# A tuned attention-and-GeGLU kernel on one core: tile 2's query transposes moved ahead of the first gates, one gate ahead of its value, and batch 2's attention one unit earlier

## Chip, cores, metric

One core of one Trainium2 chip. The metric is the device time of the kernel in microseconds (us). The traces also give the span from the first to the last instruction, which is about 2 us shorter than the time.

Engine names: PE is the matmul engine, DVE the vector engine, ACT the scalar engine, POOL and SP the two that here mostly issue or trigger transfers. A line such as L233 is a line of the kernel's source. In the views, `<-` in brackets names what ended a wait (its releaser), and DMA is a transfer between memories.

## The reference, cut

```python
# q, k, v: (8 batches, 8 heads, 576 positions, 64), float32
theta = pi / 2 * pos / S                       # S = 576
phi(x) = concat([relu(x) * cos(theta), relu(x) * sin(theta)])     # 128 features
kv  = phi(k)^T v ;  z = sum over positions of phi(k)              # per batch and head
out = (phi(q) kv) / (phi(q) z + 1e-6)
x   = out as (4608 tokens, 512)
y   = (gelu(x @ w_gate) * (x @ w_val)) @ w_out                    # d_ff = 1536
```

## The kernel before

The 4608 tokens are taken in nine blocks: block 0 is batch 0 (576 tokens), the others follow in steps of 512. A unit is one tile of 128 of the 1536 hidden columns: four gate matmuls, gelu on ACT, four value matmuls, and a product on DVE. Units are the time grid: block 1 (and each later one) has twelve, and between its units the next batch's attention is done. The kernel's PSUM is one tile, `ps`, of eight banks, and which bank a group uses is written by hand; so is the order of instructions on every engine.

```python
def norm(xb, bank, g0, g1, rows=128):          # numerator / denominator, all on DVE
    ... den = nd[..., D] + EPS                 # L181
    ... rec = 1 / den                          # L183
    ... xb[...] = nd[..., 0:D] * rec           # L184
def gate(n, jt, c0, w, gb):                    # L217: matmuls into bank gb; L222: gelu on ACT
def value(n, jt, c0, w, vb):                   # L228: matmuls into bank vb; L233: gel * value on DVE
def q_by_pe(b, j, bank, eng): ...              # L323: 8 transposes; L331/L333: copy to qT by eng
def x_by_pe(b, t, xb, bank, eng): ...          # L342: 4 transposes; L345: copy to xT by eng
def turn_x(b, t, xb): ...                      # L204: a DMA transposes xb into xT
def sq(j, which, eng): ...                     # L134 (DVE) or L136 (ACT): relu(q) * cos or sin
```

The start of block 0 (cut; "v" is DVE, "s" is ACT; X(t, bank, engine) is x_by_pe of tile t, Y(t, bank) its numerators and norm):

```python
    norm(x0, 6, 0, 1)
    dummies(1, 4)
    numer_mm(0, 0, 6, 1)
    norm(x0, 6, 1, 2)
    numer_mm(0, 1, 0, 0)
    numer_mm(0, 1, 0, 1)
    norm(x1, 0, 0, 2)
    x_by_pe(0, 0, x0, 4, "s", 0, 2)
    dummies(2, 5)
    x_by_pe(0, 0, x0, 4, "s", 2, 4)
    ...
    sq(2, 0, "v"), sq(2, 1, "s")
    gate(0, 0, 0, 128, 5)
    gate(0, 1, 0, 128, 4)
    X(1, 2, "s")()
    sq(3, 0, "v"), sq(3, 1, "v")
    dummies(1, 7)
    q_by_pe(0, 2, 3, "v")
    value(0, 0, 0, 128, 6)
    value(0, 1, 0, 128, 7)
    gate(0, 0, 128, 128, 5)
    gate(0, 1, 128, 128, 4)
    sq(4, 1, "s"), sq(4, 0, "v")
    q_by_pe(0, 3, 0, "s")
    value(0, 0, 128, 128, 6)
    value(0, 1, 128, 128, 7)
    Y(2, 2)()
    q_by_pe(0, 4, 1, "s")
    gv_unit(0, 2, *A, 4, 6)
    X(2, 0, "s")()
    ...
    X(4, 0, "v")()
    gv_unit(0, 4, *A, 3, 1)
    gv_unit(0, 2, *Bw, 4, 6)
    gv_unit(0, 3, *Bw, 5, 7)
    gv_unit(0, 0, 512, 64, 0, 3)
    gv_unit(0, 1, 512, 64, 1, 2)
```

Block 1 carries batch 2's attention (cut):

```python
    def attn_step(b, i):

        if i == 0:
            kv_half(b, 0, 6)
            kv_half(b, 1, 7)
        else:
            turn_x(b, i - 1, numer(b, i - 1, 6))
    ...
    # for n in 1..6, b = n + 1; put(u, ...) runs after unit u of block n
        put(0, L(sq, 0, 0, "v"), L(sq, 1, 0, "v"), L(sq, 1, 1, "v"), L(sq, 0, 1, "s"))
        put(1, L(sq, 2, 0, "v"), L(sq, 2, 1, "s"), L(turn_q, b, 0, 3))
        put(1, L(sq, 3, 0, "v"), L(sq, 4, 0, "v"), L(sq, 4, 1, "v"), L(sq, 3, 1, "s"), L(turn_q, b, 3, 5))
        put(2, L(sk, 0, 0, "v"), L(sk, 1, 0, "v"), L(sk, 0, 1, "s"), L(sk, 1, 1, "s"))
        put(3, L(sk, 2, 0, "v"), L(sk, 3, 0, "v"), L(sk, 4, 0, "v"))
        put(3, L(sk, 2, 1, "s"), L(sk, 3, 1, "s"), L(sk, 4, 1, "s"), L(cast_v, b, 0, 4))
        put(4, L(cast_v, b, 4, 8, "s"))
        put(5, L(attn_step, b, 0))
        ...
        for i in range(5):
            put(6 + i, L(attn_step, b, i + 1))
```

Of the kernel before, what the change touches and what calls it, by code (L numbers as in the profile page):

```python
# [16 lines left out]
def kernel(  # L17
# [19 lines left out]
    NJ = 4  # L37
# [86 lines left out]
    def dummies(n, bank=7):  # L124
        for _ in range(n):
            nc.tensor.matmul(ps[:, bank, :], lhsT=junk[:, 0:128], rhs=junk, start=True, stop=True)  # L126


    def scale(f, j, which, eng, h0=0, h1=H):
        dst, src = f  # L130
        col = (cos_c if which == 0 else sin_c)[:, j:j + 1]
        s, d = src[:, h0:h1, j, :], dst[:, j, h0:h1, which * D:(which + 1) * D]
        if eng == "v":
            nc.vector.tensor_scalar(d, s, col, 0.0, op0=ALU.mult, op1=ALU.max)  # L134
        else:
            nc.scalar.activation(d, s, AF.Relu, scale=col)  # L136
# [30 lines left out]
    def numer_mm(b, t, bank, g, rows=128):  # L167
        for h in range(4 * g, 4 * g + 4):
            nc.tensor.matmul(  # L169
                ps[0:rows, bank + g, (h % 4) * (D + 1):(h % 4 + 1) * (D + 1)],  # L170
                lhsT=qT[b % 2][:, t, h, 0:rows],
                rhs=kv[b % 2][:, h, 0:D + 1],
                start=True, stop=True,
            )

    def norm(xb, bank, g0, g1, rows=128):

        n = g1 - g0
        nd = ps[0:rows, bank + g0:bank + g1, 0:4 * (D + 1)].rearrange("p g (h e) -> p g h e", e=D + 1)
        den = rot.tile([128, 2, 4], FP32, name="den")  # L180
        nc.vector.tensor_scalar(den[0:rows, 0:n], nd[:, :, :, D], EPS, None, op0=ALU.add)  # L181
        rec = rot.tile([128, 2, 4], FP32, name="rec")
        nc.vector.reciprocal(rec[0:rows, 0:n], den[0:rows, 0:n])  # L183
        nc.vector.tensor_tensor(  # L184
            xb[0:rows, g0:g1], nd[:, :, :, 0:D],
            rec[0:rows, 0:n, :, None].to_broadcast([rows, n, 4, D]), op=ALU.mult,
        )
# [4 lines left out]
    def numer(b, t, bank, rows=128):  # L192

        numer_mm(b, t, bank, 0, rows)
        numer_mm(b, t, bank, 1, rows)
        xb = new_xb()
        norm(xb, bank, 0, 2, rows)
        return xb
# [14 lines left out]
    def gate(n, jt, c0, w, gb):  # L213

        p0 = starts[n] + c0
        for ct in range(CT):
            nc.tensor.matmul(  # L217
                ps[:, gb, 0:w], lhsT=wg_sb[:, ct, jt * 128:(jt + 1) * 128],
                rhs=xT[:, ct, p0:p0 + w], start=(ct == 0), stop=(ct == CT - 1),
            )  # L220
        gels[n, jt, c0] = gel = rot.tile([128, 512], FP32, name="gel", bufs=3)
        nc.scalar.activation(gel[:, 0:w], ps[:, gb, 0:w], AF.Gelu)  # L222

    def value(n, jt, c0, w, vb):

        p0 = starts[n] + c0
        for ct in range(CT):
            nc.tensor.matmul(  # L228
                ps[:, vb, 0:w], lhsT=wv_sb[:, ct, jt * 128:(jt + 1) * 128],
                rhs=xT[:, ct, p0:p0 + w], start=(ct == 0), stop=(ct == CT - 1),  # L230
            )
        gel = gels.pop((n, jt, c0))
        nc.vector.tensor_mul(hT[n % 2][:, jt, 64 + c0:64 + c0 + w], gel[:, 0:w], ps[:, vb, 0:w])  # L233

    def gv_unit(n, jt, c0, w, gb, vb, mid=()):
        gate(n, jt, c0, w, gb)
        for f in mid:
            f()
        value(n, jt, c0, w, vb)
# [15 lines left out]
    def o_part(n, m, bank, j0, j1):  # L255
        c0 = 128 * m - starts[n] + 64
        for jt in range(j0, j1):
            nc.tensor.matmul(  # L258
                ps[:, bank, :], lhsT=hT[n % 2][:, jt, c0:c0 + 128], rhs=wo_sb[:, jt, :],
                start=(jt == 0), stop=(jt == JT - 1),  # L260
            )
        if j1 == JT:
            o_store(m, bank)
# [21 lines left out]
    def o_store(m, bank):  # L285
        o_sb = rot.tile([128, C], FP32, name="o_sb", bufs=4)
        nc.scalar.copy(o_sb, ps[:, bank, :])  # L287
        if (128 * m) % S % 128 == 0 and (128 * m) % S < 512:
            nc.sync.dma_start(out=rows_ap(128 * m, 128), in_=o_sb)
        else:  # L290
            nc.sync.dma_start(out=rows_ap(128 * m, 64), in_=o_sb[0:64])
            nc.sync.dma_start(out=rows_ap(128 * m + 64, 64), in_=o_sb[64:128])
# [26 lines left out]
    def q_by_pe(b, j, bank, eng, h0=0, h1=H):  # L319

        qb = ps[:, bank, :].bitcast(BF16).rearrange("p (h t) -> p h t", h=H)
        for h in range(h0, h1):
            nc.tensor.transpose(out=qb[:, h, :], in_=qp[:, j, h, :], identity=ident)  # L323
        if eng is not None:
            q_evac(b, j, bank, eng, h0, h1)

    def q_evac(b, j, bank, eng, h0=0, h1=H):
        qb = ps[:, bank, :].bitcast(BF16).rearrange("p (h t) -> p h t", h=H)
        cp = nc.vector.tensor_copy if eng == "v" else nc.scalar.copy
        if j < NJ:  # L330
            cp(qT[b % 2][:, j, h0:h1], qb[:, h0:h1])  # L331
        else:
            cp(qT[b % 2][:, j, h0:h1, 0:64], qb[:, h0:h1, 0:128:2])  # L333

    def x_by_pe(b, t, xb, bank, eng, c0=0, c1=CT, every=1):
        p0 = b * S + t * 128
        cp = nc.vector.tensor_copy if eng == "v" else nc.scalar.copy
        xb2 = xb.rearrange("p g h d -> p (g h d)")
        rows = 128 if t < NJ or every == 2 else 64
        view = ps[:, bank, 0:256].bitcast(BF16).rearrange("p (c t) -> p c t", c=CT)  # L340
        for ct in range(c0, c1):
            nc.tensor.transpose(  # L342
                out=view[:, ct, 0:rows], in_=xb2[0:rows, ct * 128:(ct + 1) * 128], identity=ident[0:rows, 0:rows],
            )
        cp(xT[:, c0:c1, p0:p0 + rows // every], view[:, c0:c1, 0:rows:every])  # L345

    def sq(j, which, eng, *h):
        scale(Q, j, which, eng, *h)
# [30 lines left out]
    norm(x0, 6, 0, 1)  # L379
    dummies(1, 4)  # L380
    numer_mm(0, 0, 6, 1)
    norm(x0, 6, 1, 2)
    numer_mm(0, 1, 0, 0)
    numer_mm(0, 1, 0, 1)
    norm(x1, 0, 0, 2)
    x_by_pe(0, 0, x0, 4, "s", 0, 2)
    dummies(2, 5)
    x_by_pe(0, 0, x0, 4, "s", 2, 4)

    nc.gpsimd.tensor_copy(tiny[0:1, 1:2], x0[0:1, 1, 3, D - 1:D])  # L390
    load_w(8, 12)
# [2 lines left out]
    A, Bw = (0, 256), (256, 320)  # L394
    xs = {1: x1}

    def X(t, bank, eng):
        return lambda: x_by_pe(0, t, xs[t], bank, eng)

    def Y(t, bank):  # L400
        def f():
            xs[t] = numer(0, t, bank, 128 if t < NJ else 64)
        return f

    sq(2, 0, "v"), sq(2, 1, "s")
    gate(0, 0, 0, 128, 5)
    gate(0, 1, 0, 128, 4)
    X(1, 2, "s")()
    sq(3, 0, "v"), sq(3, 1, "v")
    dummies(1, 7)  # L410
    q_by_pe(0, 2, 3, "v")
    value(0, 0, 0, 128, 6)
    value(0, 1, 0, 128, 7)
    gate(0, 0, 128, 128, 5)
    gate(0, 1, 128, 128, 4)
    sq(4, 1, "s"), sq(4, 0, "v")
    q_by_pe(0, 3, 0, "s")
    value(0, 0, 128, 128, 6)
    value(0, 1, 128, 128, 7)
    Y(2, 2)()  # L420
    q_by_pe(0, 4, 1, "s")
    gv_unit(0, 2, *A, 4, 6)
    X(2, 0, "s")()
    Y(3, 2)()
# [5 lines left out]
    gv_unit(0, 0, 384, 128, 4, 6)  # L430
    gv_unit(0, 1, 384, 128, 5, 7)
    X(4, 0, "v")()
    gv_unit(0, 4, *A, 3, 1)
    gv_unit(0, 2, *Bw, 4, 6)
    gv_unit(0, 3, *Bw, 5, 7)
    gv_unit(0, 0, 512, 64, 0, 3)
    gv_unit(0, 1, 512, 64, 1, 2)


    load_q(1, nc.gpsimd)  # L440
# [7 lines left out]
    def L(f, *a):  # L448
        return lambda: f(*a)
# [54 lines left out]
    y4 = numer(1, 4, 0)  # L504
    o_part(0, 3, 5, 5, 10)
    x_by_pe(1, 3, y[3], 7, "s")
    o_part(0, 3, 5, 10, 12)
    x_by_pe(1, 4, y4, 6, "v", every=2)

    def attn_step(b, i):  # L510

# [8 lines left out]
    for n in range(1, 7):  # L520
        b = n + 1
        a = after[n]

        def put(u, *fs):
            a[u].extend(fs)

        put(0, L(sq, 0, 0, "v"), L(sq, 1, 0, "v"), L(sq, 1, 1, "v"), L(sq, 0, 1, "s"))
        put(1, L(sq, 2, 0, "v"), L(sq, 2, 1, "s"), L(turn_q, b, 0, 3))
        put(1, L(sq, 3, 0, "v"), L(sq, 4, 0, "v"), L(sq, 4, 1, "v"), L(sq, 3, 1, "s"), L(turn_q, b, 3, 5))
        put(2, L(sk, 0, 0, "v"), L(sk, 1, 0, "v"), L(sk, 0, 1, "s"), L(sk, 1, 1, "s"))  # L530
        put(3, L(sk, 2, 0, "v"), L(sk, 3, 0, "v"), L(sk, 4, 0, "v"))
        put(3, L(sk, 2, 1, "s"), L(sk, 3, 1, "s"), L(sk, 4, 1, "s"), L(cast_v, b, 0, 4))
        put(4, L(cast_v, b, 4, 8, "s"))
        put(5, L(attn_step, b, 0))
        if b + 1 < B:

            for f, u in zip((load_q, load_k, load_v), (3, 4, 5) if n > 1 else (6, 11, 11)):
                put(u, L(f, b + 1))
        for i in range(5):
            put(6 + i, L(attn_step, b, i + 1))  # L540

    for n in range(2, NB):
        for i, m in enumerate(o_tiles_of(n - 1)):
# [47 lines left out]
```

## Time and profile before

| | before |
|---|---|
| time, median of the first three runs | 329.17 us (328.63 to 329.31) |
| span in the trace | 326.8 us |
| PE busy / DVE / ACT | 97% / 53% / 46% |
| mean granted PE clock | 0.998 |
| PE's gaps in the list of waits | 4.3 us |

Two lines of the page: engines' busy time, and the chain that ended last.

```profile
PE 317.6 (97%) x2223; PEld 167.0 (51%) x2223; DVE 171.8 (53%) x382; ACT 150.6 (46%) x270; POOL 21.2 (6%) x41
...
PE 93%; DMA 3%; DVE 1%; ACT 1%; issue 1%; POOL 0%; SPq 0%; DVEq 0%; POOLq 0%; ACTq 0%
```

The kernel is bound by PE. The list of waits for PE in the kernel before (columns: line, what released it, total us, times, longest):

```profile
PE ps L126 <- DVE par_i L103: 1.7, 1, 1.7
PE ps L323 <- ACT qp L136: 1.0, 1, 1.0
PE ps L217 <- DMA xT<-xb: 0.8, 1, 0.8
PE ps L217 <- ACT xT L345: 0.3, 1, 0.3
PE ps L228 <- DVE hT L233: 0.2, 1, 0.2
PE ps L217 <- ACT gel L222: 0.2, 1, 0.2
```

The first two lie before 10 us and are not touched. The other four are 1.6 us together, so this change could reach only half a percent.

PE's timeline of the kernel before in block 0's beginning (start, duration, line, operation, matmuls in the group, and in brackets the idle time before it and its releaser):

```profile
15.64 0.28 PE L342 MATMUL ps<-ident,xb 128*128 128x128 bf16 x2
15.76 0.28 PE L217 MATMUL ps<-xT,wg_sb 128*128 128x128 bf16 x2
16.38 0.49 PE L217 MATMUL ps<-xT,wg_sb 128*128 128x128 bf16 x6 [0.35 <-ACT xT L345]
...
16.94 0.38 PE L126 MATMUL ps<-junk 128*128 128x512 bf16 x1
17.16 0.61 PE L323 MATMUL ps<-ident,qp 128*128 128x128 bf16 x8
...
18.05 0.61 PE L217 MATMUL ps<-xT,wg_sb 128*128 128x128 bf16 x8
18.50 0.61 PE L323 MATMUL ps<-ident,qp 128*128 128x128 bf16 x8
18.94 0.61 PE L228 MATMUL ps<-xT,wv_sb 128*128 128x128 bf16 x8
19.39 0.42 PE L169 MATMUL ps<-kv,qT 128*128 128x65 bf16 x8
```

How to read it: a group's duration runs to the modelled end of its last matmul, so groups overlap. The start-to-start distance is what counts. Eight 128-column matmuls take 18.50 - 18.05 = 0.45 us here, 56 ns each; twelve of 512 columns take 2.59 us elsewhere (306.43 to 309.02 us), 216 ns each. A single 512-column matmul is shown with 379 ns (the page's mean for L258), and the eight 128-column ones with 0.61 us. So about 0.16 us (379 - 216 ns, 0.61 - 0.45 us) of a gap behind such a group is hidden in the list of waits, and the list also leaves out what is then under 0.15 us.

PE's timeline of the kernel before at the end of block 1:

```profile
80.98 0.42 PE L169 MATMUL ps<-kv,qT 128*128 128x65 bf16 x8
...
82.10 1.03 PE L228 MATMUL ps<-xT,wv_sb 128*128 128x512 bf16 x4
83.97 1.02 PE L217 MATMUL ps<-xT,wg_sb 128*128 128x512 bf16 x4 [0.85 <-DMA xT<-xb]
```

Block 2's first gate waits until 83.97 for the DMA that turns batch 2's tile 3 (issued at 80.96, landed at 83.84 in the trace).

### The profile page before, as it was taken

To read this page: it belongs to the slowest core of one execution; us is meant where nothing else is said; L and a number is where in the kernel's file an instruction comes from. 1 tells how busy PE (TensorE), PEld (TensorE's weight loads), DVE (VectorE), ACT (ScalarE), POOL (GpSimd) and SP (SyncE) were. 2 spreads that over 40 slices of the span, in tenths; PEclk is the share of its full clock that TensorE was granted. 3 is DMA by queue.
4 is the path that set the end of the run, shared out by engine and by line. 5 is a ranking of instruction groups with operands and counts; after the bars stand their busy time and mean duration, and the time that the engine had idled before them with its cause. 6 is when DMAs were issued, how large, how long until landed. Compare 5 with 4: busy or idle time off the path is not lost.

```text
span 326.8 us, 5867 instructions
## 1 busy us (share of the span) xinstructions
PE 317.6 (97%) x2223; PEld 167.0 (51%) x2223; DVE 171.8 (53%) x382; ACT 150.6 (46%) x270; POOL 21.2 (6%) x41
## 2 busy tenths in 40 slices
PE   7799999999899999999999999999999999999994
PEld 3497866555345544544454445444544444444443
DVE  5894776678753667365835484548455222322210
ACT  6574664772474256424652375237622332223321
POOL 2640010000100010001000010001000100100000
PEclk9999999999999999999999999999999999999999
DMA  7999999997699948993699359994523211000024
GB/s 226 284 205 275 205 298 306 316 182 173 189 270 270 299 103 158 301 267 81 129 305 290 81 101 216 357 135 84 144 51 79 44 37 34 32 32 32 35 64 96
DMA packets 87739, 55.42 MB, mean 170 GB/s; under 512 B 52512, under 2 KB 82976, under 8 KB 87712
## 3 DMA queue, kind: packets, MB, share of 16 engines
q1 hardware_dynamic: 81200, 48.71, 60.2%
q0 software_dynamic: 6080, 5.90, 10.1%
q10 hardware_dynamic: 432, 0.46, 0.4%
q8 instruction: 17, 0.28, 0.4%
q14 instruction: 10, 0.08, 0.1%
HBM read 37.75 MB, written 9.44 MB: 144 GB/s over the span
## 4 chain that ended last, share of the span: by engine, by line
PE 93%; DMA 3%; DVE 1%; ACT 1%; issue 1%; POOL 0%; SPq 0%; DVEq 0%; POOLq 0%; ACTq 0%
PE ps L217 28%; PE ps L228 28%; PE ps L258 28%; PE ps L169 3%; PE ps L153 3%; DMA qf<-in_q_dram 2%; PE ps L323 1%; DMA xT<-xb 1%; PE ps L342 1%; PE ps L276 1%; DVE vx L140 0%; SPq L79 0%; DVE hT L233 0%; DVE qT L331 0%; DVE xb L184 0%
## 5 line engine op out<-in xcount | busy, mean ns | idle before, releaser
L233 DVE TENSOR_TENSOR hT<-gel,ps 128x512 bf16<-128x512 f32 (+5 forms) x126 | 76.4, 610 | 129.4 <-PE ps L228 127.8
L217 PE MATMUL ps<-xT,wg_sb 128*128 128x512 bf16 (+5 forms) x504 | 113.7, 348 | 1.4 <-DMA xT<-xb 0.8
L228 PE MATMUL ps<-xT,wv_sb 128*128 128x512 bf16 (+5 forms) x504 | 113.6, 349 | 0.2 <-DVE hT L233 0.2
L222 ACT ACTIVATE gel<-ps 128x512 f32<-128x512 f32 (+5 forms) x126 | 67.5, 536 | 77.6 <-PE ps L217 75.7
L258 PE MATMUL ps<-wo_sb,hT 128*128 128x512 bf16 x420 | 96.5, 379 | 0.0
L228 PEld LDWEIGHTS <-wv_sb 128*128 128x128 bf16 x504 | 47.8, 98 | 46.4 <-issue 0.4
L217 PEld LDWEIGHTS <-wg_sb 128*128 128x128 bf16 x504 | 45.8, 98 | 41.8 <-issue 2.1
L258 PEld LDWEIGHTS <-hT 128*128 128x128 bf16 x420 | 40.0, 98 | 45.4
L287 ACT COPY o_sb<-ps 128x512 f32<-128x512 f32 x35 | 20.5, 586 | 75.2 <-PE ps L258 75.2
L184 DVE TENSOR_TENSOR xb<-ps,rec 128x512 bf16<-128x512 f32 (+2 forms) x41 | 27.8, 678 | 1.7 <-DVE rec L183 0.2
L136 ACT ACTIVATE kp<-kf,sin_c 128x512 bf16<-128x512 f32 (+1 forms) x41 | 25.4, 679 | 0.4 <-DMA kf<-in_k_dram 0.4
L134 DVE TENSOR_SCALAR qp<-qf,cos_c 128x512 bf16<-128x512 f32 x40 | 20.5, 553 | 0.0
L169 PEld LDWEIGHTS <-qT 128*128 128x128 bf16 (+1 forms) x320 | 15.0, 98 | 8.7 <-issue 1.9
L134 DVE TENSOR_SCALAR kp<-kf,cos_c 128x512 bf16<-128x512 f32 (+1 forms) x45 | 18.7, 463 | 1.0 <-DMA kf<-in_k_dram 1.0
L136 ACT ACTIVATE qp<-qf,sin_c 128x512 bf16<-128x512 f32 x27 | 18.5, 712 | 0.0
L169 PE MATMUL ps<-kv,qT 128*128 128x65 bf16 (+1 forms) x320 | 16.5, 193 | 0.2
L208 POOL COPY xT<-xr 128x256 bf16<-128x256 bf16 x6 | 2.4, 403 | 201.0 <-DMA xr<-xb 201.0
L153 PEld LDWEIGHTS <-kp 128*128 128x128 bf16 x320 | 10.9, 97 | 2.6 <-issue 0.7
L126 PE MATMUL ps<-junk 128*128 128x512 bf16 x35 | 9.9, 424 | 1.7 <-DVE par_i L103 1.7
L153 PE MATMUL ps<-vx,kp 128*128 128x65 bf16 x320 | 11.1, 193 | 0.1
L140 ACT CAST vx<-vf 128x1280 bf16<-128x1280 f32 (+1 forms) x9 | 9.7, 1074 | 1.2 <-DMA vf<-in_v_dram 1.2
L244 POOL COPY hT<-hT 128x768 bf16<-128x768 bf16 x8 | 7.6, 948 | 36.8 <-DVE hT L233 36.8
(55 smaller groups left out, 88.9 us busy)
## 6 DMA issues: line engine op xcount, KB each, us to landing
out_dram<-o_sb SPq DMA_DIRECT2D x38, 128.0 KB, 2.4
kf<-in_k_dram SPq DMA_DIRECT2D x7, 640.0 KB, 7.5
out_dram<-o_sb SPq DMA_DIRECT2D x16, 256.0 KB, 3.4
qf<-in_q_dram SPq DMA_DIRECT2D x6, 640.0 KB, 6.2
vf<-in_v_dram SPq DMA_DIRECT2D x6, 640.0 KB, 9.1
kf<-in_k_dram SPq DMA_DIRECT2D x7, 512.0 KB, 6.4
qf<-in_q_dram SPq DMA_DIRECT2D x6, 512.0 KB, 5.4
vf<-in_v_dram SPq DMA_DIRECT2D x6, 512.0 KB, 8.0
```

Source lines behind the costliest of these rows:

```text
L126: nc.tensor.matmul(ps[:, bank, :], lhsT=junk[:, 0:128], rhs=junk, start=True, stop=True)
L134: nc.vector.tensor_scalar(d, s, col, 0.0, op0=ALU.mult, op1=ALU.max)
L136: nc.scalar.activation(d, s, AF.Relu, scale=col)
L153: nc.tensor.matmul(ps[:, bank, (h % 4) * (D + 1):(h % 4 + 1) * (D + 1)], lhsT=kp[:, j, h, :], rhs=vx[b % 2][:, j, h, 0:D + 1], start=(j == ...
L169: nc.tensor.matmul(ps[0:rows, bank + g, (h % 4) * (D + 1):(h % 4 + 1) * (D + 1)], lhsT=qT[b % 2][:, t, h, 0:rows], rhs=kv[b % 2][:, h, 0:D ...
L184: nc.vector.tensor_tensor(xb[0:rows, g0:g1], nd[:, :, :, 0:D], rec[0:rows, 0:n, :, None].to_broadcast([rows, n, 4, D]), op=ALU.mult,)
L217: nc.tensor.matmul(ps[:, gb, 0:w], lhsT=wg_sb[:, ct, jt * 128:(jt + 1) * 128], rhs=xT[:, ct, p0:p0 + w], start=(ct == 0), stop=(ct == CT - 1),
L222: nc.scalar.activation(gel[:, 0:w], ps[:, gb, 0:w], AF.Gelu)
L228: nc.tensor.matmul(ps[:, vb, 0:w], lhsT=wv_sb[:, ct, jt * 128:(jt + 1) * 128], rhs=xT[:, ct, p0:p0 + w], start=(ct == 0), stop=(ct == CT - 1),
L233: nc.vector.tensor_mul(hT[n % 2][:, jt, 64 + c0:64 + c0 + w], gel[:, 0:w], ps[:, vb, 0:w])
L258: nc.tensor.matmul(ps[:, bank, :], lhsT=hT[n % 2][:, jt, c0:c0 + 128], rhs=wo_sb[:, jt, :], start=(jt == 0), stop=(jt == JT - 1),)
L287: nc.scalar.copy(o_sb, ps[:, bank, :])
```

## The change

Three things are meant. (1) In block 0, tile 2's eight query transposes fill the wait before the first gate's second half, and a dummy matmul goes. For that the scalings of tile 2 go ahead of tile 1's norm; two copies and a scaling change engines. (2) The gate of hidden tile 4 goes ahead of its value and of two other units, and some units use other banks. (3) Six of batch 2's ten q scalings go ahead of block 1, and all its attention one unit sooner (s = -1).

```diff
--- before.py
+++ after.py
@@ -379,13 +379,16 @@
     norm(x0, 6, 0, 1)
     dummies(1, 4)
     numer_mm(0, 0, 6, 1)
+    sq(2, 1, "s")
     norm(x0, 6, 1, 2)
+    sq(2, 0, "v")
     numer_mm(0, 1, 0, 0)
     numer_mm(0, 1, 0, 1)
     norm(x1, 0, 0, 2)
     x_by_pe(0, 0, x0, 4, "s", 0, 2)
     dummies(2, 5)
     x_by_pe(0, 0, x0, 4, "s", 2, 4)
+    q_by_pe(0, 2, 3, None)
 
     nc.gpsimd.tensor_copy(tiny[0:1, 1:2], x0[0:1, 1, 3, D - 1:D])
     load_w(8, 12)
@@ -402,23 +405,21 @@
             xs[t] = numer(0, t, bank, 128 if t < NJ else 64)
         return f
 
-    sq(2, 0, "v"), sq(2, 1, "s")
     gate(0, 0, 0, 128, 5)
     gate(0, 1, 0, 128, 4)
-    X(1, 2, "s")()
-    sq(3, 0, "v"), sq(3, 1, "v")
-    dummies(1, 7)
-    q_by_pe(0, 2, 3, "v")
+    X(1, 2, "v")()
+    q_evac(0, 2, 3, "v")
+    sq(3, 0, "v"), sq(3, 1, "s")
     value(0, 0, 0, 128, 6)
     value(0, 1, 0, 128, 7)
     gate(0, 0, 128, 128, 5)
     gate(0, 1, 128, 128, 4)
     sq(4, 1, "s"), sq(4, 0, "v")
-    q_by_pe(0, 3, 0, "s")
     value(0, 0, 128, 128, 6)
     value(0, 1, 128, 128, 7)
     Y(2, 2)()
-    q_by_pe(0, 4, 1, "s")
+    q_by_pe(0, 3, 0, "s")
+    q_by_pe(0, 4, 1, "v")
     gv_unit(0, 2, *A, 4, 6)
     X(2, 0, "s")()
     Y(3, 2)()
@@ -430,11 +431,12 @@
     gv_unit(0, 0, 384, 128, 4, 6)
     gv_unit(0, 1, 384, 128, 5, 7)
     X(4, 0, "v")()
-    gv_unit(0, 4, *A, 3, 1)
+    gate(0, 4, *A, 3)
     gv_unit(0, 2, *Bw, 4, 6)
     gv_unit(0, 3, *Bw, 5, 7)
-    gv_unit(0, 0, 512, 64, 0, 3)
-    gv_unit(0, 1, 512, 64, 1, 2)
+    value(0, 4, *A, 1)
+    gv_unit(0, 0, 512, 64, 0, 2)
+    gv_unit(0, 1, 512, 64, 4, 6)
 
 
     load_q(1, nc.gpsimd)
@@ -504,8 +506,11 @@
     y4 = numer(1, 4, 0)
     o_part(0, 3, 5, 5, 10)
     x_by_pe(1, 3, y[3], 7, "s")
+    x_by_pe(1, 4, y4, 6, "v", every=2)
+    for j in range(NJ + 1):
+        sq(j, 0, "v")
     o_part(0, 3, 5, 10, 12)
-    x_by_pe(1, 4, y4, 6, "v", every=2)
+    sq(0, 1, "s")
 
     def attn_step(b, i):
 
@@ -524,20 +529,25 @@
         def put(u, *fs):
             a[u].extend(fs)
 
-        put(0, L(sq, 0, 0, "v"), L(sq, 1, 0, "v"), L(sq, 1, 1, "v"), L(sq, 0, 1, "s"))
-        put(1, L(sq, 2, 0, "v"), L(sq, 2, 1, "s"), L(turn_q, b, 0, 3))
-        put(1, L(sq, 3, 0, "v"), L(sq, 4, 0, "v"), L(sq, 4, 1, "v"), L(sq, 3, 1, "s"), L(turn_q, b, 3, 5))
-        put(2, L(sk, 0, 0, "v"), L(sk, 1, 0, "v"), L(sk, 0, 1, "s"), L(sk, 1, 1, "s"))
-        put(3, L(sk, 2, 0, "v"), L(sk, 3, 0, "v"), L(sk, 4, 0, "v"))
-        put(3, L(sk, 2, 1, "s"), L(sk, 3, 1, "s"), L(sk, 4, 1, "s"), L(cast_v, b, 0, 4))
-        put(4, L(cast_v, b, 4, 8, "s"))
-        put(5, L(attn_step, b, 0))
+        s = 0 if n > 1 else -1
+        if n > 1:
+            put(0, L(sq, 0, 0, "v"), L(sq, 1, 0, "v"), L(sq, 1, 1, "v"), L(sq, 0, 1, "s"))
+            put(1, L(sq, 2, 0, "v"), L(sq, 2, 1, "s"), L(turn_q, b, 0, 3))
+            put(1, L(sq, 3, 0, "v"), L(sq, 4, 0, "v"), L(sq, 4, 1, "v"), L(sq, 3, 1, "s"), L(turn_q, b, 3, 5))
+        else:
+            put(0, L(sq, 1, 1, "s"), L(sq, 2, 1, "v"), L(turn_q, b, 0, 3))
+            put(0, L(sq, 3, 1, "v"), L(sq, 4, 1, "s"), L(turn_q, b, 3, 5))
+        put(2 + s, L(sk, 0, 0, "v"), L(sk, 1, 0, "v"), L(sk, 0, 1, "s"), L(sk, 1, 1, "s"))
+        put(3 + s, L(sk, 2, 0, "v"), L(sk, 3, 0, "v"), L(sk, 4, 0, "v"))
+        put(3 + s, L(sk, 2, 1, "s"), L(sk, 3, 1, "s"), L(sk, 4, 1, "s"), L(cast_v, b, 0, 4))
+        put(4 + s, L(cast_v, b, 4, 8, "s"))
+        put(5 + s, L(attn_step, b, 0))
         if b + 1 < B:
 
-            for f, u in zip((load_q, load_k, load_v), (3, 4, 5) if n > 1 else (6, 11, 11)):
+            for f, u in zip((load_q, load_k, load_v), (3, 4, 5) if n > 1 else (5, 10, 11)):
                 put(u, L(f, b + 1))
         for i in range(5):
-            put(6 + i, L(attn_step, b, i + 1))
+            put(6 + s + i, L(attn_step, b, i + 1))
 
     for n in range(2, NB):
         for i, m in enumerate(o_tiles_of(n - 1)):
```

## The prediction

> **What bounds the kernel.** TensorE. The page gives PE 97% busy (317.6 of 326.8 us), the chain of waits is 93% PE, granted clock 0.998, DVE 53%, ACT 46%. [...] I use waits and start-to-start distances: almost everywhere PE's groups follow at a steady pitch (0.86 us per four 512-column matmuls). The list of waits gives PE 4.3 us of gaps: 1.7 and 1.0 before 10 us, which stay, and 0.35 (gate on ACT's copy into xT, 16.4 us), 0.24 (value on DVE's product, 25.2), 0.20 (gate on gelu, 29.6) and 0.85 (block 2's first gate, 84.0, on the DMA that turns batch 2's tile 3 into xT). So about 1.6 us, 0.5%, is all the change can reach, plus one dummy matmul.
>
> **What it does.** No real matmul goes; one 128x512 dummy does (0.22 us of pitch).
>
> 1. *Block 1 to 2.* Six q scalings of batch 2 (five on DVE at 0.40 us, one on ACT at 0.62) move ahead of block 1; all its attention runs one unit earlier (2.0 us of PE). Tile 3's transpose, issued at 80.96 and landed at 83.84 against a gate that could start at 83.12, would land near 81.9 against a gate near 82.9. The 0.85 us goes whole. Inputs allow it: q landed at 56.07, k at 60.07, v at 63.25. ACT is nearly packed from 62.5 to 70.4; its last v cast ends near 68.3 against a need near 68.9, DVE's near 67.8 against 68.3: margins of about 0.5 us. The last x tile, turned before two output matmuls, waits for its DVE product: cost about 0.1.
>
> 2. *First gates.* Tile 2's eight transposes (0.44 us) fill the 0.35 us wait; with the dummy a gain of about 0.5. But DVE runs packed there (14.0 to 25.4 with 0.34 us idle) and gets tile 1's xT copy (0.36) and tile 4's q copy (0.35) for one scaling (0.40). It waits for tile 1's transposes after a product that slipped 0.4; the first value product starts near 18.9 instead of 18.45. The second pair of values (banks 6 and 7) waits about 0.7 us on DVE, where tile 3's q transposes no longer fill. The wait at 25.2 grows to about 0.4. Net 0 to +0.3 us, I take +0.15.
>
> 3. *Gate (0,4) ahead of its value* covers the last xT copy (0.3 us); new banks trade the 0.20 at 29.6 for a wait on the late product (0.15). Net 0.
>
> Sum: -0.85 +0.10 +0.15 = -0.6 us; if the early part gains as meant, up to -1.6. All of it is on the chain, since PE is.
>
> **Prediction.** 328.4 us, 80% between 327.5 and 329.2. Faster by over 2%: 0.01; within 2%: 0.98; slower: 0.01.
>
> **Signs.** PE's list of waits no longer shows a gate on the DMA near 83 us; tile 3's transpose is issued about 2 us earlier; block 2 starts 0.6 to 1.0 us sooner; from there PE's groups are shifted by a constant. The wait at 16.4 is gone, and PE waits on DVE show near 19 (value) and 25.6. The first 256-column gate starts at 20.3 to 20.9 (before 20.21).
>
> **What would make it wrong.** The DVE wait near 19 may be smaller (then -1.3 or better). Batch 2's key-value halves may wait for casts, or qT's transposes, issued while v and outputs still land, may be late for the numerators near 71 (up to 1 us). q's second load landed at 14.27, just when ACT now wants it.

## The result

The first comparison gave 328.98 us (328.39 to 329.42, 4 runs) against 328.90 us (328.51 to 329.31, 4 runs). The ratio is 1.0001, with a 95% interval of 0.9979 to 1.0023: the same. Ratios here are the mean time of one kernel's runs over that of the other's of the same rounds, so they are not quite the ratio of the medians quoted.

The same lines of the page of the changed kernel, and its list of PE's waits:

```profile
PE 316.8 (97%) x2188; PEld 167.4 (51%) x2222; DVE 172.1 (53%) x383; ACT 150.4 (46%) x269; POOL 21.5 (7%) x41
...
PE 91%; DVE 3%; DMA 2%; issue 1%; SPq 1%; POOL 0%; ACT 0%; DVEq 0%; POOLq 0%
```

```profile
PE ps L126 <- DVE par_i L103: 1.7, 1, 1.7
PE ps L228 <- DVE hT L233: 0.8, 2, 0.6
PE ps L153 <- DVE vx L140: 0.4, 2, 0.3
PE ps L169 <- DVE xb L184: 0.3, 1, 0.3
```

Every wait that the change aimed at in block 2 and at the first gate is gone, and the list is shorter. (The missing 1.0 us of L323 and the new 0.4 us of L153 lie before 13.3 us, which the change does not touch; they come and go between traces. The changed kernel's second trace has 0.63 us of L323 again.) Yet the span is 326.7 us. PE's timeline of the changed kernel, the same places:

```profile
15.76 0.28 PE L342 MATMUL ps<-ident,xb 128*128 128x128 bf16 x2
16.14 0.62 PE L323 MATMUL ps<-ident,qp 128*128 128x128 bf16 x8
16.60 0.61 PE L217 MATMUL ps<-xT,wg_sb 128*128 128x128 bf16 x8
17.18 0.40 PE L342 MATMUL ps<-ident,xb 128*128 128x128 bf16 x4
17.41 0.61 PE L228 MATMUL ps<-xT,wv_sb 128*128 128x128 bf16 x8
18.09 0.62 PE L217 MATMUL ps<-xT,wg_sb 128*128 128x128 bf16 x8
19.28 0.61 PE L228 MATMUL ps<-xT,wv_sb 128*128 128x128 bf16 x8 [0.56 <-DVE hT L233]
19.72 0.42 PE L169 MATMUL ps<-kv,qT 128*128 128x65 bf16 x8
```

```profile
71.75 0.42 PE L169 MATMUL ps<-kv,qT 128*128 128x65 bf16 x8
...
72.87 1.03 PE L228 MATMUL ps<-xT,wv_sb 128*128 128x512 bf16 x4
74.17 0.42 PE L169 MATMUL ps<-kv,qT 128*128 128x65 bf16 x8 [0.28 <-DVE xb L184]
...
80.18 0.42 PE L169 MATMUL ps<-kv,qT 128*128 128x65 bf16 x8
...
82.16 1.03 PE L217 MATMUL ps<-xT,wg_sb 128*128 128x512 bf16 x4
...
83.89 1.03 PE L217 MATMUL ps<-xT,wg_sb 128*128 128x512 bf16 x4
```

The last gate in the second list is block 2's first one, at 83.89 us instead of 83.97: the block starts on time for its data, but no earlier.

I cut the trace at three points: the start of the second key-value half (PE, near 13.1 us), the start of hidden tile 4's 320-column gate in block 0 (the "wide gate"; first gate after the four 64-column groups), and block 2's first gate. The start point differs by up to 0.5 us between runs (12.8 to 13.3 us, by the span less the three distances). It needs the casts of v, and these v's landing: in the changed kernel DVE's second cast starts at 12.58 us after a 0.31 us wait for v's DMA, and the half at 13.20 after a 0.27 us wait for that cast. So I compare distances:

| kernel | A: key-value half to wide gate | B: wide gate to block 2 | C: block 2 to end | span |
|---|---|---|---|---|
| before | 16.57 | 54.32 | 242.81 | 326.8 |
| changed | 17.00 | 53.69 | 242.81 | 326.7 |

The change loses 0.43 us in A, gains 0.63 us in B, and nothing differs in C. The first point lay 0.12 us later in the changed kernel's run.

Where A is lost. Between 15.76 and 19.72 us PE does eight transposes and a dummy less than before (0.45 + 0.22 us), but takes 3.96 us instead of 3.75. Its start-to-start gaps are 0.27 us at 16.14, 0.13 at 17.18, 0.24 at 18.09 and 0.74 at 19.28: 1.38 us in all, against 0.51 at 16.38 before. The list of waits shows only 0.56 of it. DVE of the changed kernel in this stretch:

```profile
15.61 0.48 DVE L134 TENSOR_SCALAR qp<-qf,cos_c 128x512 bf16<-128x512 f32 x1
...
16.43 0.69 DVE L184 TENSOR_TENSOR xb<-ps,rec 128x512 bf16<-128x512 f32 x1
17.61 0.42 DVE L345 COPY xT<-ps 128x512 bf16<-128x512 bf16 x1 [0.49 <-PE ps L342]
17.95 0.68 DVE L331 COPY qT<-ps 128x1024 bf16<-128x1024 bf16 x1
18.55 0.47 DVE L134 TENSOR_SCALAR qp<-qf,cos_c 128x512 bf16<-128x512 f32 x1
18.95 0.47 DVE L233 TENSOR_TENSOR hT<-gel,ps 128x128 bf16<-128x128 f32 x2
```

All four gaps end with DVE. The scaling of tile 2, which now stands ahead of tile 1's norm, ends at 16.09 and releases the transposes at 16.14. The norm behind it ends at 17.12 (before: 16.62) and releases tile 1's transposes at 17.18. DVE then idles 0.49 us for these transposes; its copy into xT ends at 18.04 and releases the gate at 18.09. It copies and scales once more, and only then makes the product, at 18.95 (before: 18.45), which frees the bank that the value group at 19.28 writes.

So the filled wait did not become shorter: the first three gaps are 0.64 us, where 0.51 stood. The sum for A is +0.13 for these, +0.74 for the value group, -0.22 for the dummy, and -0.22 for smaller gaps after 19.4 us: +0.43.

Where B stays short of 0.85 us. The DMA wait went, but a numerator group at 74.17 now waits 0.28 us for DVE's division. DVE's product of the unit before, which the division follows, started at 72.39, though the record of its wait for PE ended at 71.97 and its gelu at 71.68. This 0.42 us pause had no cause in any semaphore that the trace shows.

### The profile page after: what moved, and what is told of

It is laid out like the page before. It is cut to its first block, busy times and chain, and to the rows that moved or that the text cites. A ratio compares the mean times of both kernels' runs of the same rounds, so it can differ in the third digit from the quotient of the medians.

```text
span 326.7 us, 5828 instructions
## 1 busy us (share of the span) xinstructions
PE 316.8 (97%) x2188; PEld 167.4 (51%) x2222; DVE 172.1 (53%) x383; ACT 150.4 (46%) x269; POOL 21.5 (7%) x41
## 4 chain that ended last, share of the span: by engine, by line
PE 91%; DVE 3%; DMA 2%; issue 1%; SPq 1%; POOL 0%; ACT 0%; DVEq 0%; POOLq 0%
PE ps L217 28%; PE ps L258 28%; PE ps L228 27%; PE ps L169 3%; PE ps L153 3%; DMA vf<-in_v_dram 2%; SPq L79 1%; DVE hT L233 1%; PE ps L276 1%; PE ps L342 1%; PE ps L323 1%; DVE xb L184 1%; DVE qp L134 0%; DVE rec L183 0%; DVE vx L140 0%
## 5 line engine op out<-in xcount | busy, mean ns | idle before, releaser
L228 PE MATMUL ps<-xT,wv_sb 128*128 128x512 bf16 (+5 forms) x492 | 111.8, 348 | 1.1 <-DVE hT L233 0.8
L217 PE MATMUL ps<-xT,wg_sb 128*128 128x512 bf16 (+5 forms) x490 | 111.8, 348 | 1.0
L258 PE MATMUL ps<-wo_sb,hT 128*128 128x512 bf16 x413 | 95.5, 379 | 0.6
L136 ACT ACTIVATE qp<-qf,sin_c 128x512 bf16<-128x512 f32 x28 | 19.3, 713 | 0.2 <-DMA qf<-in_q_dram 0.2
L153 PEld LDWEIGHTS <-kp 128*128 128x128 bf16 x320 | 10.9, 97 | 2.9 <-issue 1.0
L153 PE MATMUL ps<-vx,kp 128*128 128x65 bf16 x320 | 11.1, 193 | 0.4 <-DVE vx L140 0.4
```

Of the source, the lines that this page charges most:

```text
L136: nc.scalar.activation(d, s, AF.Relu, scale=col)
L153: nc.tensor.matmul(ps[:, bank, (h % 4) * (D + 1):(h % 4 + 1) * (D + 1)], lhsT=kp[:, j, h, :], rhs=vx[b % 2][:, j, h, 0:D + 1], start=(j == ...
L217: nc.tensor.matmul(ps[:, gb, 0:w], lhsT=wg_sb[:, ct, jt * 128:(jt + 1) * 128], rhs=xT[:, ct, p0:p0 + w], start=(ct == 0), stop=(ct == CT - 1),
L228: nc.tensor.matmul(ps[:, vb, 0:w], lhsT=wv_sb[:, ct, jt * 128:(jt + 1) * 128], rhs=xT[:, ct, p0:p0 + w], start=(ct == 0), stop=(ct == CT - 1),
L258: nc.tensor.matmul(ps[:, bank, :], lhsT=hT[n % 2][:, jt, c0:c0 + 128], rhs=wo_sb[:, jt, :], start=(jt == 0), stop=(jt == JT - 1),)
```

## The experiments

Twelve kernels, all correct. Distances as in the table above, times against the kernel before of the same rounds.

### 1. The changed kernel again

No edit.

> The changed kernel once more. Theory (early loss, late gain): block 0's first 320-column gate of ff tile 4 starts near 30.2 us again (before 29.65), block 2's first gate near 83.9 (before 83.97), time 0.0% from before within 0.15%. Rival 1 (the early loss is chance, v having landed 0.2 us later in that one profile): that gate comes back to 29.7 to 29.9. The 0.28 us wait of a numerator near 74 us follows a DVE product that started 0.42 us after its semaphores were met: if chance, it is gone here and block 2 starts near 83.6.

Measured: 328.97 against 329.00 us, ratio 0.9998 (0.9983 to 1.0013). A 17.01, B 53.68, C 242.83 us: the same to 0.02 us. The numerator's wait near 74 us came again (0.27). So neither the loss nor this wait is chance, and rival 1 falls for both. The distances repeated far better here than the times, which spread over 0.59 us in five runs (328.49 to 329.08).

### 2 and 3. Each half alone

Late part alone: the scalings ahead of block 1 and the earlier attention, put on the kernel before. Early part alone: the edits up to block 0's end.

> Before, with only batch 2's scalings and its earlier attention. Theory: nothing changes before 57 us (320-column gate at 29.65 +-0.1, block 1 at 59.6 to 59.8), no wait on the DMA into xT near 83, block 2's first gate at 83.1 to 83.4 instead of 83.97, time 0.6 to 0.85 us below before (ratio 0.9975 to 0.998). If the late part gains nothing, block 2 starts at 83.9 or later.

> Before, with only the first-gates part and the gate ahead of its value. Theory: 320-column gate at 30.1 to 30.25, block 2's first gate at 84.4 to 84.6 with its 0.85 us DMA wait kept, time 0.45 to 0.6 us above before (ratio about 1.0016). Rival 1 (chance): gate at 29.7 to 29.9 and no loss.

| kernel | time, ratio | A | B | C |
|---|---|---|---|---|
| late alone | 328.37, 0.9987 (0.9973 to 1.0001) | 16.59 | 53.69 | 242.82 |
| early alone | 329.27, 1.0013 (1.0000 to 1.0025) | 17.01 | 53.90 | 242.83 |

The parts act in their own stretches: A belongs to the early part (+0.44), B to the late one (-0.63). In the late kernel block 2's first gate came at 83.37 us, inside the forecast; both ratios alone are too near 1 to tell, so the distances carry this. Alone, the early part gets 0.42 us back in B, as the DMA wait near 84 us shrank from 0.85 to 0.42 us, the DMA landing only 0.18 us later than before (84.02 against 83.84); I had expected the wait to stay. So loss and gain are not simply added: the DMA wait was slack that absorbed 0.42 us of an earlier loss, and in the full change this slack is gone.

### 4. Tile 4's q copy back on ACT

```diff
-    q_by_pe(0, 4, 1, "v")
+    q_by_pe(0, 4, 1, "s")
```

> The changed kernel with tile 4's q copied out by ACT instead of DVE (0.60 us of DVE pitch). Theory A (DVE's throughput bounds 18 to 26 us): the product that a value waits for near 25.8 comes 0.3 to 0.6 us sooner and the 320-column gate starts at 29.6 to 29.9. Theory B (the loss is the one wait of 0.56 us at 19.3, with the filler gone): that wait lies before this copy, so the gate stays at 30.1 to 30.25.

Measured: A 17.36 us, worse than both theories allowed. ACT now has the copies of tiles 3 and 4 one after the other ahead of a gelu, which starts at 22.00 instead of 21.53 us: ACT had no room either, so this run does not tell the two theories apart. But the time was 328.40 us, ratio 0.9984 (0.9972 to 0.9997): B was 53.31 and C 242.42 us, 0.4 us less in each, in stretches that the edit does not touch. What it changes there is only that DVE's stream has one instruction less, and ACT's one more; runs 6 and 7 shift DVE's stream and leave ACT's alone. In the other five traces at that point (before, changed, again, late alone, early alone), DVE stands still for 0.39 to 0.42 us between the record before and places 191, 319 and 447 of its stream (counted from 0, records of waits included), 128 apart, and the same places in every one of them. In this one it does not.

### 5. One scaling behind the product

```diff
-    sq(3, 0, "v"), sq(3, 1, "s")
+    sq(3, 1, "s")
     value(0, 0, 0, 128, 6)
     value(0, 1, 0, 128, 7)
+    sq(3, 0, "v")
```

> The changed kernel with tile 3's first q scaling (0.40 us of DVE) moved behind the first two value products. Both theories: the value's wait at 19.3 us (0.56) shrinks to 0.1 to 0.2. Theory A (from 18 to 26 us DVE is packed, its total work sets the time): the loss comes back at the value near 25.8, whose wait grows from 0.24 to about 0.6, and the start of the fifth tile's 320-column gate less that of the second key-value half stays at 17.0 us. Theory B (the one wait at 19.3 is the loss): that distance falls to 16.6.

Measured: 328.64 against 328.77 us, ratio 0.9996 (0.9982 to 1.0010). A 16.69, B 53.69, C 242.82 us. PE's timeline of this kernel:

```profile
18.10 0.62 PE L217 MATMUL ps<-xT,wg_sb 128*128 128x128 bf16 x8
18.88 0.61 PE L228 MATMUL ps<-xT,wv_sb 128*128 128x128 bf16 x8 [0.17 <-DVE hT L233]
...
24.89 0.39 PE L217 MATMUL ps<-xT,wg_sb 128*128 128x128 bf16 x4
25.51 0.38 PE L228 MATMUL ps<-xT,wv_sb 128*128 128x128 bf16 x4 [0.24 <-DVE hT L233]
```

The wait fell by 0.39 us as both theories said, and 0.31 us of it reached the wide gate. The wait near 25.5 us did not grow. Theory A (DVE's total work bounds the stretch) falls; theory B holds: the order of one 0.40 us instruction on DVE is most of the early loss (0.31 of 0.43 us). That scaling was in front of the product that PE was waiting for, and its readers, tile 3's transposes, came only at 19.98 us.

### 6 and 7. The places on DVE's stream

On the late part alone: one tiny DVE memset added at the start, or one given to POOL.

```diff
+    pad = sb.tile([1, 2], FP32, name="pad")          # run 6 only
+    nc.vector.memset(pad, 0.0)
```

```diff
-    nc.vector.memset(kf[:, 4:8, NJ], 0.0)            # run 7 only
+    nc.gpsimd.memset(kf[:, 4:8, NJ], 0.0)
```

> Late part only, with one tiny extra DVE memset at the start, so that every later DVE instruction stands one place further on. The three 0.40 us pauses of DVE at places 191, 319 and 447 of its stream (in all traces but the one with a DVE instruction less) are then expected in front of other instructions. Theory F (the pause belongs to the place, every 128th): the product near 71.9 us starts within 0.1 us of its semaphores, the numerator's 0.28 us wait near 73.7 goes, block 2 starts 0.25 us sooner after block 1 than in the late-only run (23.71 us there). Rival G (it belongs to that instruction, through its data or semaphores): wait and distance stay.

> Late part only, with one DVE memset given to the POOL engine, so every later DVE instruction stands one place earlier. Theory F: as in the run that gave tile 4's q copy to ACT, no 0.40 us pause in front of the products near 71.9 and 212 us nor of the division near 142; block 1 to block 2 takes 23.4 to 23.5 instead of 23.71 us, and the stretch over 142 us is 0.2 us shorter; together 0.4 to 0.5 us off the late-only kernel (time near 328.0). Rival G: unchanged.

| kernel | time, ratio | A | B | C | near 142 us | tail |
|---|---|---|---|---|---|---|
| late alone (other rounds) | 328.37, 0.9987 | 16.59 | 53.69 | 242.82 | 17.08 | 15.45 |
| one place later | 328.22, 0.9986 (0.9973 to 0.9998) | 16.73 | 53.32 | 243.13 | 16.88 | 15.94 |
| one place earlier | 327.44, 0.9960 (0.9947 to 0.9974) | 16.52 | 53.32 | 242.41 | 16.88 | 15.24 |

"Near 142 us" is the distance from the 61st to the 67th gelu, the tail that from the last gelu to the end. DVE's timeline, late alone and then one place earlier:

```profile
71.88 0.69 DVE L233 TENSOR_TENSOR hT<-gel,ps 128x512 bf16<-128x512 f32 x1 [2.24 <-PE ps L169]
72.48 0.16 DVE L181 TENSOR_SCALAR den<-ps 128x8 f32<-128x8 f32 x1
...
72.91 0.69 DVE L184 TENSOR_TENSOR xb<-ps,rec 128x512 bf16<-128x512 f32 x1
```

```profile
71.48 0.69 DVE L233 TENSOR_TENSOR hT<-gel,ps 128x512 bf16<-128x512 f32 x1 [1.86 <-PE ps L228]
72.08 0.16 DVE L181 TENSOR_SCALAR den<-ps 128x8 f32<-128x8 f32 x1
...
72.51 0.69 DVE L184 TENSOR_TENSOR xb<-ps,rec 128x512 bf16<-128x512 f32 x1
```

In the first, the product starts 0.42 us after its wait record ended and ACT had long been done; in the second it starts 0.05 us after it. In both kernels the numerator's wait is gone and B is 0.37 us shorter. Theory F holds against rival G: the 0.42 us pause did not stay with the product (place 575, below, shows it stay with a place). With the shift, what stands at places 191, 319 and 447 is an instruction whose predecessor is still running, or a wait, and no such pause is to be seen there.

The tail moves too: place 575 in the late kernel is DVE's last drain (in the trace of the kernel before it starts at 326.45 us and takes 0.12 us, and the closing semaphore records of POOL and then of the other engines follow from 326.60 us on), and it stands 0.45 us after the record before; one place earlier that drain follows after 0.09 us, and it is the next record, now at place 575, that stands 0.46 us behind its predecessor: there the pause is seen at the same place, in front of another instruction.

The later shift made the tail 0.49 us longer, which I did not foresee. In its trace the drain no longer pauses, but the last two output transfers, issued at the same distance from the last gelu, land 0.82 and 0.71 us later than in the late kernel (14.55 and 14.73 us after that gelu's start, where all thirteen other traces have 13.73 to 13.75 and 14.01 to 14.03). Whether the shift has to do with these landings is not shown. Its A grew by 0.14 us: a smaller pause at place 63 (0.15 us) stands in front of the first instruction of tile 2's norm and no longer of the second, and the transposes behind that norm came 0.14 us later relative to the groups before.

### 8. Tile 3's x copy on ACT

On the late part alone:

```diff
-    X(3, 1, "v")()
+    X(3, 1, "s")()
```

> Late part only, and in block 0 the copy of tile 3's turned x by ACT instead of DVE (0.36 us off DVE, where ACT has 0.95 us idle). Theory A (DVE bounds to 26 us): the value's 0.24 us wait at 25.3 goes, the 320-column gate starts 0.2 to 0.25 us sooner (distance from the second key-value half 16.35 instead of 16.59). Theory B: that wait is due to the banks, and stays.

Measured: 327.89 against 328.77 us, ratio 0.9969 (0.9957 to 0.9982). A 16.75, B 53.32, C 242.41 us. The forecast failed: the value's 0.24 us wait stayed although DVE had 0.36 us less to do before it, and A did not shrink, as the gate near 29.6 waited 0.36 us for its gelu instead of 0.20. So the wait near 25 us is a ring, from PE through DVE back to PE: a group of numerators, its norm (1.10 us from its start to the product's, in the traces of both kernels), the product behind it, the bank that this frees. The wait was 0.24 us in this run as in runs 1 to 5, whatever DVE had to do before. As for the gelu, ACT's stream is one instruction longer here, and this gelu stands at its place 63 (62 in late alone): it starts 0.18 us after the gelu before it ended, 0.01 in late alone. That looks like DVE's small pause at place 63, but this one trace does not show that it is. The gain in B and C is that of run 7, for here too DVE's stream is one instruction shorter from block 0 on.

### 9 and 10. The same place shift on before and on the changed kernel

The edit of run 7.

> The kernel before with only the one DVE memset given to POOL (DVE's stream one place earlier). If the places of the 0.40 us pauses are worth what the late-only pair showed: nothing changes up to block 2 (its 0.85 us wait on the DMA into xT stays or is 0.4 to 0.9), the stretch over 142 us takes 16.88 instead of 17.07 us and the tail 15.24 instead of 15.45; 0.4 us less in all, time near 0.9988 of before. If the gain of 0.8 us came only together with the late part, time is within 0.0005 of before.

> The changed kernel with the same memset given to POOL. Expected: the numerator's 0.28 us wait near 74 goes (block 1 to block 2 in 23.3 to 23.4 us instead of 23.70), and 0.2 and 0.2 us at 142 us and in the tail; the early part's 17.0 us stays. About 0.65 us below the changed kernel, time near 0.998 of before.

| kernel | time, ratio | A | B | C |
|---|---|---|---|---|
| before, one place earlier | 328.27, 0.9983 (0.9971 to 0.9996) | 16.51 | 54.18 | 242.40 |
| changed, one place earlier | 328.05, 0.9977 (0.9964 to 0.9991) | 17.00 | 53.31 | 242.41 |

C falls by 0.4 us in both, with or without the change. Taken between these two, without the pause, the late part is worth 0.87 us in B, about the 0.85 us forecast, and the early part still costs 0.49 in A.

### 11. Scalings ahead, attention not

```diff
-        s = 0 if n > 1 else -1
+        s = 0
```

> The changed kernel with batch 2's scalings ahead of block 1 but its attention in the old units. Theory (the DMA wait goes because the numerators come one unit sooner): the wait into xT near 84 us is there again (0.4 to 0.9 us), no numerator wait near 74, block 1 to block 2 takes 23.9 to 24.4 us, time 0.0005 to 0.0020 above before. If the earlier scalings alone free DVE and the transposes, the distance is 23.7 or less.

Measured: 329.23 against 328.84 us, ratio 1.0012 (0.9999 to 1.0026). A 16.99, B 54.26, C 242.83 us; PE's wait for the DMA into xT is back (0.78 us), the numerator's is gone. Scaling q sooner gives nothing by itself. The gain is the unit by which the numerators, and the DMA after them, come earlier.

### 12. What the runs point to

Late part, one DVE place earlier, no early part, and in block 0:

```diff
-    dummies(1, 7)
...
-    gv_unit(0, 1, 384, 128, 5, 7)
+    gv_unit(0, 1, 384, 128, 5, 3)
...
-    gv_unit(0, 4, *A, 3, 1)
+    gv_unit(0, 4, *A, 7, 1)
...
-    gv_unit(0, 1, 512, 64, 1, 2)
+    gv_unit(0, 1, 512, 64, 4, 6)
```

> Late part, the DVE stream one place earlier, and in block 0 three PE waits taken away by other banks: the value that waits 0.24 us near 25 writes bank 3, the gate that waits 0.2 us near 29.6 finds bank 1 long free; and one dummy matmul is left out. Expected: second key-value half to the 320-column gate in 16.05 to 16.2 us (16.59 before), neither wait shown, the rest as in the late kernel with one DVE place less; span 324.8 to 325.0 us, time 1.7 to 1.9 us below before (ratio 0.9943 to 0.995).

Measured: 327.05 us against 328.84, ratio 0.9946 (0.9933 to 0.9958). A 15.96, B 53.32, C 242.42 us. PE's list of waits:

```profile
PE ps L126 <- DVE par_i L103: 1.5, 1, 1.5
PE ps L153 <- DVE vx L140: 0.4, 1, 0.4
PE ps L217 <- ACT xT L345: 0.3, 1, 0.3
```

It is 0.5% faster than the kernel before (the changed kernel, which was not in these rounds, equals that one in run 1), below the 2% that would be called faster, but its interval is clear of 1. The distance A fell by 0.56 us from run 7, a little more than forecast; how much each of the edits gave was not tested. The ring near 25 us no longer shows a wait, since the value writes another bank and does not need the product of two groups before.

## Why the prediction was right or wrong

- *PE bounds the kernel, and about 1.6 us of waits can be reached: right.* Nothing here moved the time by more than 0.6%.
- *The time: inside the range, but the forecast gain did not appear.* 328.98 us against 328.4 (327.5 to 329.2). Of -0.6 us, -0.20 is left in the distances (+0.43 and -0.63), and the first cut lay 0.12 us later, which it does between traces of one kernel too (13.20 and 13.29 us in the two of the changed kernel). The number is inside because the range also holds the time of the kernel before (328.90 in these rounds): that is luck, or width, and no sign that the sum was right.
- *"The 0.85 us goes whole": the wait did, the gain did not.* B gained 0.63 us. The term that I left out is a pause of DVE at a place of its stream. Before, place 191 was the product of unit 5, at 70.63 us, where the key-value halves followed and the product waited for its gelu until 70.48 anyway. With the attention one unit sooner, the same product stands in front of a norm that PE waits for: 0.28 us. Runs 7, 9 and 10 show the pause and, without it, 0.87 us.
- *The early part, "+0.15": the waits on DVE were foreseen, the gain was not there.* The first product was forecast near 18.9 (18.95), the value's wait at 0.7 us (0.56 shown, 0.74 from start to start), the first 256-column gate at 20.3 to 20.9 (20.87). The step that failed is the fill, "with the dummy a gain of about 0.5". The dummy gave its 0.22 us, but the gaps around the first gates went from 0.51 to 0.64 us and did not vanish: the transposes that fill the wait need a scaling on DVE, and with it ahead of tile 1's norm, tile 1's transposes and its gate waited too. "The wait at 25.2 grows to about 0.4" was wrong as well: it stayed at 0.24 us, in favour of the change. Runs 5 and 8 show that this wait is a ring of fixed length (0.24 us in both) which slides with its start. The forecast's own terms (-0.5, +0.7, +0.16) add up to +0.36 us, nearer the measured 0.43 than the 0.15 that was taken.
- *Gate (0,4) ahead of its value, net 0: right within what the trace shows.* From that late value to the wide gate it took 4.36 us instead of 4.42.
- *The x tile turned before two output matmuls, "about 0.1": not seen.* From the wide gate to block 1's first gate both kernels take 29.99 us.
- *The margins of 0.5 us of the casts, and qT's transposes: held.* No key-value half of batch 2 and no numerator waited for them in the trace of the changed kernel.
- *Tile 3's transpose "about 2 us earlier": wrong*, 80.15 against 80.96 us. From block 1's first gate to batch 2's first key-value half it is 8.63 us instead of 10.36, so one unit is 1.73 us and not 2.0; the early loss and the numerator's wait took the rest.
- *"Block 2 starts 0.6 to 1.0 us sooner": wrong*, 0.08 us; *"from there groups are shifted by a constant": right*, C is equal to 0.02 us.
- Open: why the early-alone kernel's DMA landed only 0.18 us later when it was issued 0.60 us later. In both traces tile 2's transpose, issued before it, landed at 83.2 us (83.17 and 83.21), and tile 3's 0.67 and 0.81 us after that, so its landing followed tile 2's and not its own issue; what held tile 2's is not shown. Open too: what makes DVE pause, and the late landings in run 6.

## What to carry to other kernels

When PE is bound by short waits, count from start to start: matmul durations in a trace overlap, and here they hid 0.8 us of gaps spread over four groups while the list of waits grew shorter. Before filling one engine's wait with moved work, look at what the move puts in front of the instruction that the bound engine needs next: a 0.40 us scaling ahead of a product cost 0.31 us, another ahead of a norm left the filled wait as long as it was, and a wait that is a ring of dependencies passed the delay on and did not absorb it (0.24 us at 25.23 us before, 0.24 us at 25.84 us in the changed kernel). And when a small reordering gives an odd sum, shift the helper engine's stream by one harmless instruction: in this kernel one place earlier alone was worth about as much as the whole late part (0.61 to 0.86 us in A, B and C together, in three pairs of traces).
